# A second seven-product unit beside the first in one tile, weight sums moved between tiles, and two small copies on another engine

## The chip, the cores and the metric

The kernel runs on one core of a Trainium2 chip. The metric is the device time of one execution in microseconds (us). A core has a matrix engine (TensorE, PE in the profile, with its weight loads shown as PEld), a vector engine (VectorE, DVE), a scalar engine (ScalarE, ACT), GpSimd (POOL) and SyncE (SP); each works through its own queue in order, and they wait for each other on semaphores.

## The reference, cut to what matters

Attention over 8 batches of 8 heads, with keys and values pooled by 8 along the sequence, then a feed-forward layer with SiLU between its two products:

```python
k_p = k.reshape(B, H, Sp, 8, D).mean(axis=3)       # B, H, S, D = 8, 8, 576, 64; Sp = 72
v_p = v.reshape(B, H, Sp, 8, D).mean(axis=3)
attn = softmax(q @ k_p.T / sqrt(D))
x = (attn @ v_p) as rows of tokens                  # 4608 x 512
h = x @ w_in                                        # 512 x 2048
g = h * (1.0 / (1.0 + np.exp(-h)))
out = g @ w_out                                     # 2048 x 512, float32
```

## The kernel before

The 4608 tokens are cut into nine tiles of 512, numbered t = 0 to 8. For each tile `up` computes the hidden activations `h_T` (16 groups of 128 hidden units) from `xT`, and `down` or `down_quarters` multiplies them with `w_out` and stores. The attention of the next batch is laid between the matmuls of the current tile.

**The order.** All order is written out by hand. `up` and `down` advance a counter before each small set of matmuls (`next(step)`), and lists of fillers, `f_up` and `f_down`, hold pairs (step, work). `spread` sorts them by step, keeping the order of equals, and issues a filler once the counter has passed its step; what is left is issued at the end. Since every engine takes its work in the order of issue, the step of a filler sets its place in that engine's queue.

**up.** `items` lists what `up` does. A plain group `(g, 0, 512)` is four matmuls of 512 columns into a bank of PSUM, then one SiLU on ScalarE (lines 537 and 543); it counts four steps. The other kind is a unit: four hidden groups (`UNITS`: groups 4 to 7, 8 to 11, 12 to 15) made with seven products instead of eight, in the manner of Strassen and Winograd. In `items` a unit is named by its number and a string of digits, each digit one product of four matmuls of 256 columns (line 477) and two steps. Around the products of a unit stand these operations, in one queue each:

- after 2: ScalarE copies bank P to `r_sb` (line 494); after 5: VectorE adds Q to it, `rr_sb` (497); after 1: VectorE makes `t_sb` from R (500);
- 4 goes on in bank P and 3 in bank Q, each followed by a SiLU from the bank (485);
- 7 goes on in P and 6 in Q, each followed by a VectorE sum into `c_sb[0]` or `c_sb[1]` (509, 512), and "h" and "s" are the SiLUs of those two (485).

Thus 4 waits for the copy, 3 for `rr_sb`, 7 and 6 for the SiLUs of 4 and 3. `r_sb`, `rr_sb`, `t_sb` and `c_sb` exist once and are used by all units. Banks P and Q come from a ring of five ("at"), which the attention uses too, R and the plain groups from a ring of three ("mm"). Tiles 2 to 8 run three units interleaved and four plain groups (the strings `THREE`). Tile 0 has plain groups only. Tile 1 runs one unit (number 0) and twelve plain groups. A unit takes sums of weights, `w_sum1`, built once on VectorE by `unit_weight_sum`: those of units 0 and 1 while tile 0 is in `down`, those of unit 2 in tile 1.

**down.** Tile 0 uses plain products (`down`, line 572). From tile 1 on `down_quarters` uses seven products of 16 matmuls each (line 645), in the order 2, 5, 1, 4, 3, 7, 6, with sums of hidden activations (`h_sum`, `hidden_sum`, line 605, from VectorE) and sums of output weights (`w_sum`, `weight_sum`, line 623). Each weight sum n has PW = 4 parts of two k-groups; its parts are fillers. Sums 1 and 3 are made in tile 0's `down`, sums 4, 7 and 6 in tile 1's `up`. The last tile (`last`) goes over the products 1, 4, 3, 7, 6 twice, once for each half `cc` of its rows; there the bank P is copied to `o_sb[1]` between products 4 and 7 by VectorE (line 667), in the other tiles by ScalarE.

**ScalarE's tables.** `attn_tables` (line 400) loads the set with Exp and Ln, `moe_tables` (403) the set with SiLU; `moe_tables` is issued just before `up`.

**Other lines that are spoken of.** 159: `q_transpose`; 292 and 310: the copies of pooled keys and values to SBUF (`kz`, `vp`); 263 and 267: sums of the loaded rows (`slot_sums`); 393: the attention's result into `xT`; 437, 444: the sums of unit weights and of x; 384: numerators; 358: denominators; 340: scores. `w_out` is loaded in four pieces of four k-groups (`load_w_out`, line 731), pieces 0 to 2 before batch 1's values and piece 3 after them.

Of the kernel before, what the change touches and what calls it, by code (L numbers as in the profile page):

```python
# [36 lines left out]
def kernel(  # L37
# [9 lines left out]
    nc = tc.nc  # L47
# [43 lines left out]
    def ps_tile(shape, dtype, tag, name):  # L91
        return psum.tile(shape, dtype, tag=tag, bufs=banks[tag], name=name)
# [16 lines left out]
    o_sb = [singles.tile([128, 2, d_model], FP32, name=f"o_sb{n}") for n in range(2)]  # L109
# [204 lines left out]
    def part(g, f):  # L314
        return ((g, f * QF, (f + 1) * QF),)
# [36 lines left out]
    def denominators(b, segs, on_dve=False):  # L352
        st = batches[b]
        w = width(segs)
        es = st["es", segs]
        den_ps = ps_tile([128, 512], FP32, "at", "den_ps")
        for s in range(4):
            nc.tensor.matmul(  # L358
                den_ps[32 * s : 32 * (s + 1), :w],
                lhsT=ones, rhs=es[:, s, :], start=True, stop=True,  # L360
            )
        rec = mid.tile([128, VW], FP32, tag="rec", bufs=4, name="rec")[:, :w]
        if on_dve:
            nc.vector.reciprocal(rec, den_ps[:, :w])
        else:
            lnd = mid.tile([128, VW], FP32, tag="lnd", name="lnd")[:, :w]
            nc.scalar.activation(lnd, den_ps[:, :w], func=AF.Ln)  # L367
            nc.scalar.activation(rec, lnd, func=AF.Exp, scale=-1.0)
        st["rec", segs] = rec
# [32 lines left out]
    def moe_tables():  # L402
        nc.scalar.preload_act_table_set("silu_and_others")


    def spread(fillers, n):
        todo = sorted(fillers, key=lambda f: f[0])
        for i in range(n):
            yield i
            while todo and todo[0][0] <= i:  # L410
                todo.pop(0)[1]()
        for f in todo:
            f[1]()
# [28 lines left out]
    def unit_x_sum(t, n):  # L442
        a, b = U_X[n]
        nc.vector.tensor_tensor(  # L444
            out=x_sum[:, U_XI[n]], in0=x_quarter(t, *a), in1=x_quarter(t, *b),
            op=ALU.subtract if n in (3, 4) else ALU.add,
        )
# [97 lines left out]
    def store(t, m, cs, engines=(nc.sync,)):  # L545
        n0 = (t * NTT + m * 128) // QP
        src = o_sb[m // 2][:, m % 2, cs]
        if n0 // QI == B - 1:
            engines[0].dma_start(out=out[n0 * QP : n0 * QP + 128, cs], in_=src)  # L549
            return  # L550
        for u in range(128 // QP):
            n = n0 + u
            rows = (
                out[n * QP : (n + 1) * QP] if n // QI == B - 1
                else out_r[n // QI, n % QI]
            )
            engines[u % len(engines)].dma_start(
                out=rows[:, cs], in_=src[QP * u : QP * (u + 1)]
            )
# [27 lines left out]
    LO, HI, FULL = slice(0, CQ), slice(CQ, 2 * CQ), slice(0, 2 * CQ)  # L587
# [30 lines left out]
    PW = 4  # L618
# [6 lines left out]
    def left(n, kt, c):  # L625
        cs = slice(128 * c, 128 * (c + 1))
        if n in h_sum:
            return h_sum[n][:, kt, cs]
        i = n - 3
        return h_T[:, i * KQ + kt, i * NQ + 128 * c : i * NQ + 128 * (c + 1)]  # L630

    def down_quarters(t, fillers, last=False):
        step = spread(fillers, 7 * 2 * KQ)
        ps = {
            n: ps_tile([128, 2, CQ], FP32, "mm", f"o_ps{n}") for n in "PQR"
        }
        bank = {2: "P", 5: "Q", 1: "R", 4: "P", 3: "Q", 7: "P", 6: "Q"}
        begun = set()

        def product(n, k0, k1, cs=(0, 1)):  # L640
            b = bank[n]
            for kt in range(k0, k1):
                for c in cs:
                    next(step)
                    nc.tensor.matmul(  # L645
                        ps[b][:, c, :], lhsT=left(n, kt, c), rhs=W_OUT[n][:, kt, :],
                        start=b not in begun,
                        stop=kt == k1 - 1, skip_group_check=True,
                    )
                    begun.add(b)  # L650

        add, sub = ALU.add, ALU.subtract
        tt = nc.vector.tensor_tensor
        KA = KQ // 2
        product(2, KA, KQ)
        product(5, KA, KQ)
        product(2, 0, KA)
        nc.scalar.copy(r_sb, ps["P"])
        product(5, 0, KA)
        tt(out=rr_sb, in0=ps["Q"], in1=r_sb, op=add)  # L660
        for cc in ((0,), (1,)) if last else ((0, 1),):
            cs = slice(cc[0], cc[-1] + 1)
            product(1, 0, KQ, cc)
            tt(out=t_sb[:, cs], in0=ps["R"][:, cs], in1=rr_sb[:, cs], op=sub)
            product(4, 0, KQ, cc)
            copy = nc.vector.tensor_copy if last else nc.scalar.copy
            copy(o_sb[1][:, cs, LO], ps["P"][:, cs])
            tail = last and cc == (1,)
            if tail:
                store(t, 3, LO, (nc.gpsimd,))  # L670
            product(3, 0, KQ, cc)
            nc.vector.tensor_copy(out=o_sb[0][:, cs, HI], in_=ps["Q"][:, cs])
            if tail:
                store(t, 1, HI)
            product(7, 0, KQ, cc)
            tt(out=o_sb[0][:, cs, LO], in0=ps["P"][:, cs], in1=t_sb[:, cs], op=add)
            for c in cc:
                store(t, c, LO if tail else FULL, (nc.scalar if tail else nc.sync,))
            product(6, 0, KQ, cc)
            tt(out=o_sb[1][:, cs, HI], in0=ps["Q"][:, cs], in1=t_sb[:, cs], op=add)  # L680
            for c in cc:
                if tail:
                    store(t, 3, HI, both)
                else:
                    store(t, 2 + c, FULL, (nc.gpsimd if last else nc.sync,))
        for _ in step:
            pass
# [105 lines left out]
    for t in range(NT):  # L793
        a = t + 1
        f_up, f_down = [], []
        if t == 0:
            GA = 11
            items = [(g, 0, HS) for g in range(GA)]
            items += [(g, HS, NTT - HS) for g in range(GA)]
            items += [(g, 0, NTT) for g in range(GA, KG)]  # L800
            f_up += [(1, lambda: denominators(0, part(0, 1), on_dve=True))]
            f_up += [(5, lambda: denominators(0, part(1, 1), on_dve=True))]
            f_up += [(13, lambda: numerators(0, part(0, 1)))]
            f_up += [(17, lambda: numerators(0, part(1, 1)))]
        else:
            G = lambda *gs: [(g, 0, NTT) for g in gs]
            if t == 1:
                items = (
                    G(12, 13, 14, 15) + [(0, "251")] + G(8) + [(0, "43")] + G(9)
                    + [(0, "7h6")] + G(10) + [(0, "s")] + G(11, 0, 1, 2, 3)  # L810
                )
            else:
                items = []
                for it in THREE[t // B].split():
                    items += [(("BCA".index(it[0])), it[1])] if it[0] in "ABC" else G(int(it[1]))
            if t == 1:
                for n in U_X:
                    f_up.append((0, lambda n=n: unit_x_sum(t, n)))
            for n in (2, 5):
                h_at = 50 if t == B else 54 if t > 1 else 45  # L820
                f_up.append((h_at, lambda n=n: hidden_sum(n, 4, 8)))
            f_up.append((56, lambda: hidden_sum(6, 4, 8)))
            for n, k0 in ((2, 0), (5, 0), (1, 4), (1, 0)):
                f_up.append((64, lambda n=n, k0=k0: hidden_sum(n, k0, k0 + 4)))
            f_down.append((33, lambda: hidden_sum(7, 0, 8)))
            f_down.append((71 if t < B else 50, lambda: hidden_sum(6, 0, 4)))

        for n, t0, f_to, at, parts in (
            (1, 0, f_down, 48, (0, PW)), (3, 0, f_down, 52, (0, PW)),
            (4, 1, f_up, 38, (0, PW)), (7, 1, f_up, 42, (0, PW)),  # L830
            (6, 1, f_up, 60, (0, PW)),
        ):
            for i in range(*parts):
                if t == t0:
                    f_to.append((at + i, lambda n=n, i=i: weight_sum(n, i)))
# [63 lines left out]
        if t == 1:  # L899
# [5 lines left out]
            f_down.append((72, unit_weight_tiles))  # L905
            for i, n in enumerate(U_W):
                f_down.append((73 if i < 2 else 81, lambda n=n: unit_weight_sum(2, n)))
        moe_tables()
        up(t, f_up, items)
        if t == 0:  # L910
            down(t, f_down, [(0, 1, 2), (3,)])
        else:
            down_quarters(t, f_down, last=t == NT - 1)
# [28 lines left out]
```

The softmax here doesn't subtract the row's maximum and nothing guards it: scores larger than these inputs give would overflow.

## Time and profile before

| what | value |
|---|---|
| median of 6 runs | 280.61 us (280.35 to 281.25) |
| the profiled execution | 280.63 us, of which the span is 278.6 us |
| granted TensorE clock | 1.000 |
| busy share PE / PEld | 98% / 73% |
| busy share DVE / ACT / POOL | 79% / 68% / 35% |
| chain that ended last, PE's share | 94% |
| tile 0's `down`, tile 1's `up`, tile 1's `down` | about 32.6 to 50.9, 50.9 to 65.0 and 65.0 to 81.2 us |

The time of an execution is the span (first to last instruction) and about 2 us around it. Lines of the timeline are: start, duration, engine, source line and operation, output and inputs by the program's names, form, count, and in brackets the idle time before it with what ended that. In the lines of waits the three numbers are the total, the count and the longest. In the chain each line is a start, a length and what the chain went through.

### The profile page before, as it was taken

What the parts mean: (1) busy time and instruction counts of PE and PEld (TensorE: products, weight loads), DVE (VectorE), ACT (ScalarE), POOL (GpSimd) and SP (SyncE); (2) the same over time, 40 slices, a digit from 0 to 9 for tenths busy, and PEclk for the clock granted to TensorE, in tenths of its full rate; (3) what the DMA queues carried; (4) which work ended last, traced back from release to release, by engine and by line L of the source; (5) the groups of instructions that cost most, each with busy time, mean ns of one, the idle gap of its engine ahead of it and who ended that gap; (6) DMA issues with size and microseconds to landing.
All of it is one profiled execution on the core that took longest, in us unless ns stands there. A gap on an engine that the chain in (4) does not pass through costs nothing.

```text
span 278.6 us, 7101 instructions
## 1 busy us (share of the span) xinstructions
PE 272.7 (98%) x2845; PEld 202.9 (73%) x2865; DVE 218.8 (79%) x413; ACT 188.2 (68%) x366; POOL 98.3 (35%) x104
## 2 busy tenths in 40 slices
PE   8999999999999999999999999999999999999995
PEld 4448444556778677867888788687877778788784
DVE  4886737889998976897689768986888588966983
ACT  1688765668577966797679757985799478326700
POOL 8745217332148430953086107970630000000001
PEclk9999999999999999999999999999999999999999
DMA  7999999897669878669755835599610041005004
GB/s 215 276 254 244 207 326 195 227 186 116 133 84 211 216 111 149 143 175 136 135 141 152 129 57 133 142 126 134 145 46 2 2 107 46 0 12 141 1 7 146
DMA packets 31312, 37.70 MB, mean 135 GB/s; under 512 B 10352, under 2 KB 22256, under 8 KB 31280
## 3 DMA queue, kind: packets, MB, share of 16 engines
q0 software_dynamic: 23920, 27.03, 52.5%
q1 hardware_dynamic: 6928, 9.58, 12.3%
q10 hardware_dynamic: 432, 0.66, 0.7%
q8 instruction: 22, 0.36, 0.5%
q14 instruction: 10, 0.08, 0.1%
HBM read 36.70 MB, written 9.44 MB: 166 GB/s over the span
## 4 chain that ended last, share of the span: by engine, by line
PE 94%; DVE 2%; ACT 1%; issue 1%; DVEq 0%
PE hp_ps L537 16%; PE o_psP L645 16%; PE o_psQ L645 16%; PE u_psQ L477 10%; PE u_psP L477 10%; PE o_psR L645 5%; PE sc_ps L340 4%; PE o_ps L572 3%; PE u_psR L477 3%; PE warm_ps L694 3%; PE nu_ps L384 3%; PE den_ps L358 2%; PE warm_ps L698 1%; DVE w_sum L623 1%; DVE xT L393 1%
## 5 line engine op out<-in xcount | busy, mean ns | idle before, releaser
L645 PEld LDWEIGHTS <-h_sum 128*128 128x128 bf16 x640 | 60.6, 98 | 11.9 <-DVE h_sum L605 1.5
L537 PE MATMUL hp_ps<-xT,w_in_sb 128*128 128x512 bf16 (+3 forms) x269 | 51.4, 332 | 1.0 <-issue 0.2
L605 DVE TENSOR_TENSOR h_sum<-h_T 128x1024 bf16<-128x1024 bf16 (+1 forms) x72 | 49.7, 744 | 0.0
L477 PEld LDWEIGHTS <-w_sum 128*128 128x128 bf16 x440 | 43.0, 98 | 7.8
L348 ACT ACTIVATE es<-sc_ps 72x384 bf16<-72x384 f32 (+1 forms) x100 | 39.0, 469 | 8.5 <-PE sc_ps L340 8.3
L543 ACT ACTIVATE h_T<-hp_ps 128x512 bf16<-128x512 f32 (+2 forms) x67 | 33.8, 524 | 11.5 <-PE hp_ps L537 9.8
L537 PEld LDWEIGHTS <-w_in_sb 128*128 128x128 bf16 x284 | 27.0, 98 | 17.1 <-issue 1.1
L485 ACT ACTIVATE h_T<-c_sb 128x512 bf16<-128x512 f32 x44 | 27.5, 628 | 3.1 <-DVE c_sb L509 2.4
L393 DVE TENSOR_TENSOR xT<-nu_ps,rec 128x384 bf16<-128x384 f32 (+1 forms) x50 | 24.0, 533 | 4.3 <-PE nu_ps L384 4.3
L645 PEld LDWEIGHTS <-h_T 128*128 128x128 bf16 x256 | 24.1, 98 | 4.5 <-issue 0.9
L549 POOL DMA_DIRECT2D out_dram<-o_sb x2 | 1.2, 617 | 68.2 <-issue 67.4
L367 ACT ACTIVATE lnd<-den_ps 128x384 f32<-128x384 f32 (+1 forms) x23 | 11.1, 483 | 20.0 <-PE den_ps L358 20.0
L190 POOL TENSOR_TENSOR raw<-raw 72x1024 f32<-72x1024 f32 x10 | 23.6, 2360 | 0.1
L500 DVE TENSOR_TENSOR t_sb<-u_psR,rr_sb 128x512 f32<-128x512 f32 x22 | 15.2, 692 | 7.0 <-PE u_psR L477 5.5
L494 ACT COPY r_sb<-u_psP 128x512 f32<-128x512 f32 x22 | 12.9, 585 | 10.0 <-PE u_psP L477 8.7
L263 DVE TENSOR_TENSOR raw<-raw 128x384 f32<-128x384 f32 (+3 forms) x20 | 12.4, 618 | 8.6 <-DMA raw<-in_v_dram 4.8
L477 PEld LDWEIGHTS <-w_in_sb 128*128 128x128 bf16 x176 | 16.9, 98 | 2.3
L645 PE MATMUL o_psP<-w_out_sb,h_sum 128*128 128x256 bf16 x128 | 17.6, 273 | 0.0
L497 DVE TENSOR_TENSOR rr_sb<-u_psQ,r_sb 128x512 f32<-128x512 f32 x22 | 15.0, 680 | 2.9 <-ACT r_sb L494 1.6
L509 DVE TENSOR_TENSOR c_sb<-u_psP,t_sb 128x512 f32<-128x512 f32 x22 | 15.1, 688 | 2.7 <-PE u_psP L477 1.0
L512 DVE TENSOR_TENSOR c_sb<-u_psQ,t_sb 128x512 f32<-128x512 f32 x22 | 15.1, 687 | 2.3 <-PE u_psQ L477 2.2
L196 POOL COPY gate<-x_sum 1x1 bf16<-1x1 bf16 x5 | 0.9, 180 | 45.3 <-DVE x_sum L444 45.3
(84 smaller groups left out, 525.8 us busy)
## 6 DMA issues: line engine op xcount, KB each, us to landing
out_dram<-o_sb SPq DMA_DIRECT2D x128, 64.0 KB, 1.7
raw<-in_k_dram POOLq DMA_DIRECT2D x10, 576.0 KB, 8.0
raw<-in_v_dram POOLq DMA_DIRECT2D x10, 576.0 KB, 7.8
q_bf<-in_q_dram POOLq DMA_DIRECT2D x6, 576.0 KB, 10.7
w_in_sb<-in_moe_w_in_dram POOLq DMA_DIRECT2D x8, 256.0 KB, 8.7
w_out_sb<-in_moe_w_out_dram POOLq DMA_DIRECT2D x4, 512.0 KB, 13.2
raw<-in_v_dram POOLq DMA_DIRECT2D x2, 768.0 KB, 10.9
raw<-in_k_dram POOLq DMA_DIRECT2D x1, 768.0 KB, 10.8
```

The source lines that it names most:

```text
L190: nc.gpsimd.tensor_add(out=raw[:, :, : 2 * D], in0=raw[:, :, : 2 * D], in1=raw[:, :, 2 * D :])
L348: nc.scalar.activation(es[:, s, :], sc[s], func=AF.Exp, scale=score_scale)
L393: nc.vector.tensor_mul(out=xT[:, 2 * g0 + c : 2 * (g0 + ng - 1) + c + 1 : 2, cols], in0=nu[c][:, :w].rearrange("r (g n) -> r g n", g=ng), ...
L477: nc.tensor.matmul(ps[y, bank][:, u, :], lhsT=w[:, kk, 128 * u : 128 * (u + 1)], rhs=x[:, kk, :], start=first and u == 0 and kk == 0, stop ...
L485: nc.scalar.activation(h_T[:, g : g + 2, j * NQ : (j + 1) * NQ], src, func=AF.Silu)
L500: tt(out=t_sb, in0=ps[y, "R"], in1=rr_sb, op=ALU.subtract)
L509: tt(out=c_sb[0], in0=ps[y, "P"], in1=t_sb, op=ALU.add)
L512: tt(out=c_sb[1], in0=ps[y, "Q"], in1=t_sb, op=ALU.add)
L537: nc.tensor.matmul(hp_ps[:, r0:r1], lhsT=w_in_sb[:, kk, g * 128 : (g + 1) * 128], rhs=xT[:, kk, x0 : x0 + r1 - r0], start=(kk == 0), stop= ...
L543: nc.scalar.activation(h_T[:, g, n0 : n0 + n], hp_ps[:, :n], func=AF.Silu)
L605: nc.vector.tensor_tensor(out=h_sum[n][:, ks, :], in0=quarter(*a, ks), in1=quarter(*b, ks), op=op)
L645: nc.tensor.matmul(ps[b][:, c, :], lhsT=left(n, kt, c), rhs=W_OUT[n][:, kt, :], start=b not in begun, stop=kt == k1 - 1, skip_group_check= ...
```

## The change

Tile 1 runs unit 1 beside unit 0, so that four plain groups fewer (8 to 11) remain; its `items` are a new order. Of the output weight sums, all of 6 and the first halves of 4 and 7 are issued in tile 0's `down`, at steps 8 to 15, and the second halves of 4 and 7 in tile 1's `down`, at steps 22, 23 and 54, 55; none is left in tile 1's `up`. The load of the SiLU tables for tile 1 is issued at step 46 of tile 0's `down` instead of after it. In the last tile ScalarE makes the copies of line 667.

```diff
@@ down_quarters
-            copy = nc.vector.tensor_copy if last else nc.scalar.copy
-            copy(o_sb[1][:, cs, LO], ps["P"][:, cs])
+            nc.scalar.copy(o_sb[1][:, cs, LO], ps["P"][:, cs])
@@ for t in range(NT), t == 1
                 items = (
-                    G(12, 13, 14, 15) + [(0, "251")] + G(8) + [(0, "43")] + G(9)
-                    + [(0, "7h6")] + G(10) + [(0, "s")] + G(11, 0, 1, 2, 3)
+                    G(12, 13, 14, 15) + [(0, "25143"), (1, "2"), (0, "7"), (1, "5")]
+                    + [(0, "6h"), (1, "1"), (0, "s")] + G(0) + [(1, "43")] + G(1)
+                    + [(1, "7h6")] + G(2) + [(1, "s")] + G(3)
                 )
@@ weight sums: (n, tile, list, first step, parts)
             (1, 0, f_down, 48, (0, PW)), (3, 0, f_down, 52, (0, PW)),
-            (4, 1, f_up, 38, (0, PW)), (7, 1, f_up, 42, (0, PW)),
-            (6, 1, f_up, 60, (0, PW)),
+            (6, 0, f_down, 8, (0, PW)), (4, 0, f_down, 12, (0, 2)),
+            (7, 0, f_down, 14, (0, 2)), (4, 1, f_down, 20, (2, PW)), (7, 1, f_down, 52, (2, PW)),
@@
-        moe_tables()
+        if t != 1:
+            moe_tables()
+        if t == 0:
+            f_down.append((46, moe_tables))
         up(t, f_up, items)
```

## The prediction

> **What bounds the kernel now.** First the page: engine shares and the chain that ended last.
>
> ```profile
> PE 272.7 (98%) x2845; PEld 202.9 (73%) x2865; DVE 218.8 (79%) x413; ACT 188.2 (68%) x366; POOL 98.3 (35%) x104
> ...
> PE 94%; DVE 2%; ACT 1%; issue 1%; DVEq 0%
> ```
>
> TensorE's queue is the chain, at full clock, so an edit counts only if it takes TensorE work away or changes one of its waits. The change touches four places: tile 0's `down` (32.6 to 50.9 us), tile 1's `up` (50.9 to 65.0), tile 1's `down` (65.0 to 81.2), the last tile's `down`. I read the timeline of each. Tile 0's:
>
> ```profile
> 30.68 3.40 DVE L437 TENSOR_TENSOR w_sum<-w_in_sb 128x512 bf16<-128x512 bf16 x10
> ...
> 37.01 0.73 POOL L151 DMA_DIRECT2D q_bf<-in_q_dram  x1 [2.00 <-DMA w_out_sb<-in_moe_w_out_dram]
> ...
> 38.92 1.55 DVE L263 TENSOR_TENSOR raw<-raw 128x768 f32<-128x768 f32 x2 [4.84 <-DMA raw<-in_v_dram]
> ...
> 46.56 0.59 ACT L580 COPY o_sb<-o_ps 128x512 f32<-128x512 f32 x1
> ```
>
> VectorE ends the ten unit weight sums at 34.08 and is idle for 4.84 us until batch 1's values land. GpSimd's wait shows that the third piece of `w_out` was there by 37.01. After 47.15 ScalarE is idle for 3.97 us.
>
> Then tile 1's `up`, VectorE and ScalarE (a later mean over several instructions hides their spacing, which is given below):
>
> ```profile
> 55.28 0.58 ACT L494 COPY r_sb<-u_psP 128x512 f32<-128x512 f32 x1
> ...
> 57.30 0.51 DVE L292 CAST kz<-kz_ps 128x144 bf16<-128x144 f32 x2
> 57.73 1.19 DVE L159 STREAM_TRANSPOSE qT<-q_bf 128x288 f32<-128x288 f32 x3
> 59.63 0.69 DVE L509 TENSOR_TENSOR c_sb<-u_psP,t_sb 128x512 f32<-128x512 f32 x1 [0.71 <-ACT h_T L485]
> ...
> 66.65 2.50 DVE L605 TENSOR_TENSOR h_sum<-h_T 128x1024 bf16<-128x1024 bf16 x4
> ```
>
> TensorE does not wait in this `up` after 52.0. But VectorE falls behind: from 59.63 to the end of `vp` at 73.43 it has no idle time, and in tile 1's `down` TensorE waits for it twice:
>
> ```profile
> PEld L645 <- DVE h_sum L605: 0.2, 1, 0.2
> PEld L384 <- DVE vp L310: 0.2, 1, 0.2
> ```
>
> At the end, the chain of the last tile and VectorE's copy of line 667:
>
> ```profile
> 268.32 0.87 PE o_psQ L645 x8
> 269.20 0.01 issue
> 269.21 1.03 PE o_psP L645 x8
> 270.24 0.93 PE o_psQ L645 x8
> ```
>
> ```profile
> 268.74 0.42 DVE L667 COPY o_sb<-o_psP 128x256 f32<-128x256 f32 x1
> ```
>
> Eight matmuls take 0.87 (the first line), so 1.03 and 0.93 hold waits of 0.17 and 0.06: product 7 overwrites bank P, which VectorE has read only at 269.16, since it was on `h_sum` of product 7 (267.27 to 268.49) and `t_sb` before.
>
> **Part 1, tile 0's down: nothing.** Eight weight sums at 0.336 spacing (of 0.42 each, overlapped; 2.76 for eight at 46.67) take 2.7 of the idle 4.84. The four of sum 6 need pieces 0 and 1 of `w_out`, the other four piece 2: in the worst case from 37.01, 4 x 0.336 and one tail, to 38.4; batch 1's values are awaited until 38.92. Behind stand the values' sums and then `select_v`, for which TensorE has 0.66 us more (sums end 42.25, select at 42.91). Without that cover it would be up to 2.7 us. The table load moves past the copies of row blocks 2 and 3 on ScalarE. It delays the first and its stores on SP by 1.28 us, to 48.4; the bank is wanted for a group after 50.9 and `o_sb[1]` after 74, so nobody waits. It starts tile 1's first SiLUs 0.9 us sooner, but TensorE did not wait for those: the SiLU of the fourth group (54.79) already waited for TensorE, as would the copy to `r_sb` at 55.28. Worth 0.
>
> The Trainium skill (ScalarE: Activation LUTs, What ACT_TABLE_LOAD costs) speaks of a drain of about 1.38 us behind each load, 2.66 us in all. Here the load of line 403 started at 51.72, took 1.28, and the SiLU followed at 53.01, so no drain is seen. By the page the copy would end at 49.9 instead of 48.4, with the same sum.
>
> **Part 2, tile 1's up.** Out: 16 matmuls of 512 columns at 0.216 spacing, 3.45 us. In: 28 of 256 at 0.109, 3.06. TensorE saves 0.39 if it never waits. VectorE loses 12 weight sums (4.0 us), but gains four f32 sums of unit 1 (0.69, next one after 0.60, 0.11 later where it reads the one before); ScalarE gives four SiLUs of plain groups for a copy and four SiLUs.
>
> I walked the three queues with these spacings (ScalarE 0.49, 0.53 after a SiLU from `c_sb`; a semaphore about 0.04). A2, A5, A1 (unit 0 = A, unit 1 = B) end as before, and `t_sb` runs from 56.69. The keys' matmuls (0.43) now fall inside A4, so TensorE passes A3 at 57.20, B2 57.64, A7 58.07, B5 58.51, A6 58.95, B1 59.38, G0 60.25, B4 60.69, B3 61.12, G1 61.99. VectorE: two `kz`, three transposes until 58.8, then c7 of A 58.8, `rr_sb` of B 59.4, c6 of A 60.0 to 60.7, `t_sb` of B 60.6 to 61.3. ScalarE: SiLU of c6 from 60.75, and behind it G0's, which was ready at 60.4, from 61.28, B4's 61.77 to 62.37, B3's to 62.86. So B7 can't start at 61.99 but at 62.42, and B6 after it waits to 62.91: **0.43 + 0.05 us of new waits**. G2 and G3 follow and `down` starts at 65.08 instead of 64.98: **+0.09** net instead of -0.39. The waits are the least known term. Below: 0, if the transposes or sums run more overlapped. Above: every late 0.1 us of c6 is passed on in full; 1.2 if c6 comes 0.75 later than walked (a whole copy of 0.58 and a few hand-overs). I take 0.48, as all its terms are rows of this tile.
>
> **Part 3, tile 1's down.** G3's SiLU ends at about 66.02 and the four sums of `h_sum` start at 66.05 instead of 66.65, since no weight sum stands before them. The wait before `h_sum` goes: spacing of matmuls at 67.2 to 67.4 was 0.207 against 0.109, **-0.10**. Steps 22 and 23 put two weight sums (0.67) before `vp`: it ends at 73.43 - 0.60 + 0.67 = 73.50, and the numerators wait for it: **+0.07** on their time of before. Behind the latter pair (steps 54, 55) stand `xT`, `h_sum` 6 and unit 2's weights; VectorE is then 0.74 us later, and had 0.92 us idle at 76.2, so it is even by the copy at 77.14. The scores at 76.03 need a bank that `xT` frees at 75.2. Together: TensorE comes to the numerators 0.01 sooner (+0.09 - 0.10) and waits there until 0.07 after its time of before, so tile 1 ends **0.07 later**.
>
> **Part 4, last tile.** Product 4's first half ends at 268.33. ScalarE is idle from 266.4; 128x256 f32 lies between its rows of 72x256 (0.359) and 128x512 (0.586), nearer the first: 0.37. So P is free at 268.75 (269.0 at the upper bound), and product 7 could start at 269.04. VectorE's copy of Q moves to 269.34 to 269.76, before product 6 at 269.91. Both waits go: **-0.23**. In the second half nothing waited. ScalarE's store there is behind its copy by over 1 us. The bounds are 0 and -0.23.
>
> **Sum.** Against the profiled execution, 280.63 = 278.65 + 1.98: +0.07 - 0.23 = -0.16, so 280.47; it lies 0.02 over the median of 280.61, so **280.45**. Differences within 0.2% (0.56 us) are about what a measurement of this kernel can tell from no change.
>
> **Rivals.**
> *Faster: unit 1 runs without waits.* -0.39 - 0.10 - 0.23, and some hundredths less wait for `vp`: about -0.75, 279.85. For it: tiles 2 to 8 run three units with no wait of TensorE in `up`. Against: there at most one transpose stands between the sums of units. Chance 0.22.
> *Slower: ScalarE's queue closes in tile 1.* B's copy to `r_sb` stands behind two SiLUs (of A4 and A3), and with VectorE in order the sum `rr_sb` of B takes c6 of A with it, and c6 its SiLU, G0's, B4's and so B7. If this slips by 0.75 beyond the walk (c6 ends at 61.5 or later, the point from which it decides), `up` costs +0.84; `h_sum` starts at 66.80 and `vp` ends at 73.43 + 0.15 + 0.67 = 74.25, so tile 1 ends 0.82 late; less 0.23 at the tail: +0.6, 281.2. Against: the walk has the copy done at 58.5, 0.9 before VectorE is free for it. Chance 0.18.
> *No use of ScalarE's copy:* the tail stays, as product 7 waits elsewhere; +0.07, 280.68. About 0.1, inside "same".
> *Weight sums hold the values back in tile 0:* would need the third piece later than 37.5; the values are behind it on the same queue and landed two microseconds after it. Under 0.03.
>
> **How the numbers follow.** Same: 0.60 (forecast 0.5, dead tail 0.1). Faster 0.22, slower 0.18 are the two waits' ends. The range runs from 279.8 (no waits) to 281.2 (closed queue); the likeliest case alone has 280.2 to 280.75.
>
> **What would show it.** Right: DVE's 4.84 us before line 263 shrinks to under 1.5; in tile 1's `up` TensorE waits about 0.4 us before u_psP of B7, released by ScalarE's line 485; `h_sum` leaves the waits of PEld in tile 1, `vp` stays; `down` of tile 1 starts near 65.1; the last tile's 1.03 and 0.93 become 0.87. Wrong: `down` before 64.7 or after 65.7, or a stall at 38 to 43 us.

## The result, and the profile after

The changed kernel takes **279.98 us** (median of 34 runs, 279.81 to 280.73) against 280.51 of the kernel before (70 runs); the ratio is 0.9981, 95% interval 0.9976 to 0.9986: 0.53 us less, just inside the 0.2% that I called no change. The forecast was 280.45.

The stages can be compared by the starts of TensorE's first instruction in each, read from the timelines of the two profiled executions (us):

| stage | before | after | forecast of the difference |
|---|---|---|---|
| tile 0's `down` | 18.27 | 18.27 | 0 |
| tile 1's `up` | 14.07 | 14.10 | +0.09 |
| tile 1's `down` | 16.17 | 16.13 | -0.02 |
| tiles 2 to 7, tile 8's `up` | 181.75 | 181.75 | 0 |
| tile 8's `down`, to the last matmul | 12.64 | 12.41 | -0.23 |
| last matmul to the end of the span | 3.10 | 3.11 | 0 |
| outside the span | 1.98 | 1.78 | 0 |

The profiled execution after took 280.99 us, above the median, since its first product of tile 0's `down` came 0.79 later (33.44 instead of 32.65). That is in a part of the program that the change does not touch; all times of after below stand 0.79 later than the like ones of before.

Tile 0, timeline of after:

```profile
34.50 1.43 DVE L623 TENSOR_TENSOR w_sum<-w_out_sb 128x512 bf16<-128x512 bf16 x4
...
37.33 1.43 DVE L623 TENSOR_TENSOR w_sum<-w_out_sb 128x512 bf16<-128x512 bf16 x4 [1.40 <-DMA w_out_sb<-in_moe_w_out_dram]
...
39.87 1.55 DVE L263 TENSOR_TENSOR raw<-raw 128x768 f32<-128x768 f32 x2 [1.11 <-DMA raw<-in_v_dram]
```

VectorE's 4.84 us before line 263 have become four weight sums, a wait of 1.40 for the third piece of `w_out`, four more sums and a wait of 1.11. The sums of line 263, which wait for the values to land, start 0.16 later after the first product than before (6.43 instead of 6.27), and TensorE does not feel it: tile 0's `down` takes its 18.27.

Tile 1's `up`, the chain of after around product 7 of unit 1 (B7):

```profile
60.88 0.61 DVE c_sb L512
61.49 0.02 issue
61.51 0.63 ACT h_T L485
62.14 0.48 ACT h_T L543
62.62 0.49 ACT h_T L485
63.12 0.04 issue
63.16 0.60 PE u_psP L477 x4
```

This is the queue of the walk: c6 of unit 0, its SiLU, G0's, B4's, then B7. On VectorE c7 and c6 of unit 0 (lines 509 and 512) stand behind the three transposes:

```profile
58.52 1.19 DVE L159 STREAM_TRANSPOSE qT<-q_bf 128x288 f32<-128x288 f32 x3
59.63 0.65 DVE L509 TENSOR_TENSOR c_sb<-u_psP,t_sb 128x512 f32<-128x512 f32 x1
60.20 0.68 DVE L497 TENSOR_TENSOR rr_sb<-u_psQ,r_sb 128x512 f32<-128x512 f32 x1
60.80 0.67 DVE L512 TENSOR_TENSOR c_sb<-u_psQ,t_sb 128x512 f32<-128x512 f32 x1
```

G1's last matmul gave way at 62.79, so B7 waited 0.37 (walk: 0.43), and B6 0.05 more. The list of waits names the releaser, and `vp` is still there while `h_sum` is gone from TensorE's waits in this tile:

```profile
PEld L384 <- DVE vp L310: 0.2, 1, 0.2
...
PE u_psP L477 <- ACT h_T L485: 0.2, 1, 0.2
```

The last tile, chain and timeline of after (the copy is line 666 now):

```profile
269.99 0.87 PE o_psP L645 x8
270.87 0.87 PE o_psQ L645 x8
```

```profile
269.15 0.37 ACT L666 COPY o_sb<-o_psP 128x256 f32<-128x256 f32 x1 [2.00 <-PE o_psP L645]
```

ScalarE's copy took 0.37 and both waits, 0.17 and 0.06, are gone.

So from tile 0's first `down` product to the end of the span the two profiles differ by 0.23 us, all in the last tile; tile 1 is even (30.23 us in both). What the medians have beyond that was the question for the experiments.

### The profile page after: what moved, and what is told of

Its sections match the earlier page's. It is cut to its first block, busy times and chain, and to the rows that moved or that the text cites. A ratio compares the mean times of both kernels' runs of the same rounds, so it can differ in the third digit from the quotient of the medians.

```text
span 279.2 us, 7140 instructions
## 1 busy us (share of the span) xinstructions
PE 272.1 (97%) x2857; PEld 203.8 (73%) x2877; DVE 220.8 (79%) x415; ACT 189.4 (68%) x369; POOL 98.3 (35%) x104
## 4 chain that ended last, share of the span: by engine, by line
PE 88%; DVE 4%; DMA 3%; ACT 2%; issue 1%; POOL 0%; POOLq 0%; DVEq 0%
PE o_psQ L645 16%; PE o_psP L645 15%; PE hp_ps L537 15%; PE u_psP L477 11%; PE u_psQ L477 10%; PE o_psR L645 5%; PE sc_ps L340 4%; PE o_ps L572 3%; PE u_psR L477 3%; DMA raw<-in_v_dram 3%; PE nu_ps L384 3%; PE den_ps L358 2%; DVE w_sum L623 1%; DVE xT L393 1%; ACT h_T L543 1%
## 5 line engine op out<-in xcount | busy, mean ns | idle before, releaser
L645 PEld LDWEIGHTS <-h_sum 128*128 128x128 bf16 x640 | 60.7, 98 | 11.5 <-DVE h_sum L605 1.3
L477 PEld LDWEIGHTS <-w_sum 128*128 128x128 bf16 x460 | 45.0, 98 | 8.4 <-issue 0.5
L537 PE MATMUL hp_ps<-xT,w_in_sb 128*128 128x512 bf16 (+3 forms) x253 | 47.8, 329 | 0.8
L543 ACT ACTIVATE h_T<-hp_ps 128x512 bf16<-128x512 f32 (+2 forms) x63 | 31.6, 520 | 9.9 <-PE hp_ps L537 7.9
L537 PEld LDWEIGHTS <-w_in_sb 128*128 128x128 bf16 x268 | 25.6, 98 | 15.3 <-issue 1.1
L485 ACT ACTIVATE h_T<-c_sb 128x512 bf16<-128x512 f32 x46 | 28.8, 629 | 4.4 <-DVE c_sb L509 3.1
L500 DVE TENSOR_TENSOR t_sb<-u_psR,rr_sb 128x512 f32<-128x512 f32 x23 | 15.9, 692 | 6.7 <-PE u_psR L477 5.0
L477 PEld LDWEIGHTS <-w_in_sb 128*128 128x128 bf16 x184 | 17.6, 98 | 2.4
L497 DVE TENSOR_TENSOR rr_sb<-u_psQ,r_sb 128x512 f32<-128x512 f32 x23 | 15.7, 681 | 3.5 <-ACT r_sb L494 1.6
L512 DVE TENSOR_TENSOR c_sb<-u_psQ,t_sb 128x512 f32<-128x512 f32 x23 | 15.8, 687 | 2.3 <-PE u_psQ L477 2.1
L509 DVE TENSOR_TENSOR c_sb<-u_psP,t_sb 128x512 f32<-128x512 f32 x23 | 15.8, 686 | 2.2 <-PE u_psP L477 0.9
L645 PE MATMUL o_psQ<-w_sum,h_sum 128*128 128x256 bf16 x128 | 16.7, 273 | 0.0
```

The source lines that it names most:

```text
L477: nc.tensor.matmul(ps[y, bank][:, u, :], lhsT=w[:, kk, 128 * u : 128 * (u + 1)], rhs=x[:, kk, :], start=first and u == 0 and kk == 0, stop ...
L485: nc.scalar.activation(h_T[:, g : g + 2, j * NQ : (j + 1) * NQ], src, func=AF.Silu)
L500: tt(out=t_sb, in0=ps[y, "R"], in1=rr_sb, op=ALU.subtract)
L509: tt(out=c_sb[0], in0=ps[y, "P"], in1=t_sb, op=ALU.add)
L512: tt(out=c_sb[1], in0=ps[y, "Q"], in1=t_sb, op=ALU.add)
L537: nc.tensor.matmul(hp_ps[:, r0:r1], lhsT=w_in_sb[:, kk, g * 128 : (g + 1) * 128], rhs=xT[:, kk, x0 : x0 + r1 - r0], start=(kk == 0), stop= ...
```

## The experiments

Each kernel is compared with runs of the kernel before on the same chip. The theory: tile 1 gives nothing because of B7's wait, the last tile gives 0.23, and the rest is not work of the schedule. The rival: one of the parts gives 0.3 us that the profiled executions don't show.

### Each part alone

```diff
 tail_alone:   only   copy(...) -> nc.scalar.copy(o_sb[1][:, cs, LO], ps["P"][:, cs])
 sums_alone:   only   the five rows of weight sums as in the change
 tables_alone: only   moe_tables at step 46 of tile 0's down
 unit_alone:   only   the new items of tile 1
```

tail_alone: 

> Only the last tile's copies of line 667 go to ScalarE; all else as before. By the walk: both waits of the last tile go, 0.23 us less (ratio 0.9992), and the last tile's chain shows 0.87 in place of 1.03 and 0.93. Rival (the part of the gain that the two profiles do not show lies in the last tile, in its stores or around the span): 0.5 us less (0.9982).

sums_alone: 

> Only the weight sums move: sum 6 and half of 4 and 7 to tile 0's down, the other halves to tile 1's down; tile 1 keeps one unit. By the walk: the wait for h_sum goes (0.10) and the one for vp shrinks by about 0.1: 0.1 to 0.2 us less (0.9993 to 0.9996); tile 0 no longer. Rival (the hidden gain lies in the weight sums): 0.4 to 0.5 less. Third case (tile 0 pays): 0.3 or more slower, with a wait of TensorE at 38 to 44 us.

tables_alone: 

> Only the load of the SiLU tables moves from behind tile 0's down to its step 46. By the walk: nothing (1.0000), as TensorE does not wait for the first SiLUs. Rival (most executions, other than the profiled one, do wait for those SiLUs): 0.3 us less (0.9990).

unit_alone: 

> Only tile 1's items change: unit 1 beside unit 0, with the weight sums 4, 7 and 6 still in that up and the tables and the copies as before. By the walk: eight parts of sums 4 and 7 (2.7 us) stand on VectorE before the hidden sums and c7 of unit 1, four of sum 6 before the last hidden sums, so h_sum comes about 1.9 us late for product 2's second half: 1.5 to 2 us slower (1.005 to 1.007). Rival (weight sums were no load): same as before within 0.1.

| kernel | median us | ratio to before (95%) | tile 0 `down` | tile 1 `up` | tile 1 `down` | tile 8 `down` | last matmul to end of span | outside the span |
|---|---|---|---|---|---|---|---|---|
| tail_alone | 280.52 | 0.9999 (0.9991 to 1.0008) | 18.27 | 14.06 | 16.16 | 12.41 | 3.68 | 1.79 |
| sums_alone | 280.44 | 0.9997 (0.9988 to 1.0005) | 18.78 | 14.07 | 16.00 | 12.71 | 3.11 | 1.98 |
| tables_alone | 280.40 | 0.9999 (0.9991 to 1.0008) | 18.27 | 14.06 | 16.16 | 12.64 | 3.10 | 1.94 |
| unit_alone | 282.10 | 1.0058 (1.0046 to 1.0070) | 18.27 | 14.10 | 17.90 | 12.64 | 3.10 | 1.79 |

(The stages are from each kernel's profiled execution, the time outside the span is the mean of time less span over all its runs.)

**The unit alone** costs 1.76 us in tile 1, as walked. The weight sums left in its `up` hold VectorE until the last hidden sums, which start at 68.30 instead of 66.65:

```profile
66.96 1.43 DVE L623 TENSOR_TENSOR w_sum<-w_out_sb 128x512 bf16<-128x512 bf16 x4
68.30 2.49 DVE L605 TENSOR_TENSOR h_sum<-h_T 128x1024 bf16<-128x1024 bf16 x4
```

So moving the sums is what makes the second unit affordable. **The sums alone** take 0.17 out of tile 1's `down`, as expected; the list of waits there has neither `h_sum` nor `vp`. Their time shows little of it. In the profiled execution tiles 2 to 8 took 0.14 more (181.82 and 12.71), for a reason that was not looked for, and tile 0's `down` was 0.51 longer, for which the chain gives the reason:

```profile
27.01 16.17 DMA w_out_sb<-in_moe_w_out_dram
```

TensorE waited for the fourth piece of `w_out`, which landed at 43.19. **The tables alone** do nothing, although the first SiLU came at 52.05 instead of 53.01. **The tail alone** saves its 0.23 before the last matmul and loses 0.58 behind it: its last store landed 2.76 us after the last matmul, in the other three 2.18 or 2.19. It measured as before. The interval excludes the rival's 0.9982 but still holds the 0.9992 of the walk, which had the saving right and knew nothing of the loss. By the means of all runs its span is 0.16 longer than that of the kernel before (278.75 and 278.58), and the time outside the span is 0.19 shorter.

### The changed kernel without its tail, and the tail once more

```diff
 after_no_tail: the changed kernel with
+            copy = nc.vector.tensor_copy if last else nc.scalar.copy
+            copy(o_sb[1][:, cs, LO], ps["P"][:, cs])
 tail_again: tail_alone unchanged
```

after_no_tail: 

> The changed kernel with VectorE's copy back in the last tile: unit, sums and tables remain. Theory (tile 1 is even, the last tile is the gain inside the span): 0.2 us slower than the changed kernel, last tile's chain with 1.03 and 0.93 again; the time outside the span stays at 1.79 if it goes with the unit's program, since the unit alone had 1.79 also. Rival (the tail is worth nothing, as the tail alone measured the same as before): same as the changed kernel, 280.0.

tail_again: 

> The tail alone once more, one look: in its first profile the last store landed 2.27 us after its issue ended beside 1.36 before, 0.58 more than anywhere else, which took the tail's 0.23 back. If that belongs to the kernel, it is there again; if to that execution, the last store lands after 2.18 us from the last matmul, and the span ends 3.1 us after it.

Without its tail the changed kernel takes 280.53 (ratio to before 1.0001, 0.9991 to 1.0011): 0.55 more than with it, where 0.2 was expected. Tile 1 (14.10 and 16.14) is as in the changed kernel, the last `down` 12.64 again, so 0.23 is the tail's. The rest is not in these stages: in its profiled execution tile 0's `down` took 18.58, and by the means of all runs its span is 0.50 longer than that of the changed kernel (278.82 and 278.32). The time outside the span stayed at 1.78, with the unit and without the tail.

The tail once more had its late landing again, at 2.57: it belongs to that kernel. In the trace's DMA packets a single packet of 8 KB of instruction code (queue 14) stands beside it, 1.24 us after the last matmul (1.23 in tail_alone), for 0.56 and 0.72 us. In the kernel before such a packet comes 4.82 us after the last matmul, which is after the span; in the changed kernel 3.67 us before it. Page of before, then of after:

```profile
q14 instruction: 10, 0.08, 0.1%
```

```profile
q14 instruction: 11, 0.09, 0.1%
```

One more piece of code is fetched within the span after the change. Counted over the traces, the packet's place goes with the number of ScalarE's instructions: 444 in before, sums_alone and tables_alone (4.8 to 5.0 after the last matmul); 446 in unit_alone and after_no_tail (4.1 to 4.4 after); 450 in tail_alone (1.2 after); 452 in the changed kernel (3.7 before). And the time outside the span is 1.94 to 1.98 with 444, 1.78 to 1.79 in all of these others. (Instructions of the sequencer are counted.) That gave a new theory: about 0.2 us of the gain is where the last code fetch falls. Whether it falls inside the span can't be what counts, since the span ends 3.10 after the last matmul: in unit_alone and after_no_tail the packet comes behind its end too, and the time outside is 1.79 and 1.78. By the place of the fetch, what counts would be whether it comes by 4.4 us after the last matmul or only at 4.8.

### The code fetch moved by idle copies

```diff
 before_pad: the kernel before, tail_pad: tail_alone, each with
+    pad = singles.tile([128, 1], FP32, name="pad")
+            if t == 0:
+                for _ in range(8):        # 4 in tail_pad
+                    f_down.append((46, lambda: nc.scalar.copy(pad, warm32[:, :1])))
```

before_pad: 

> The kernel before with eight more copies of one column each on ScalarE, at step 46 of tile 0's down, where ScalarE is idle; they compute nothing that is used. Theory (0.19 us of the change's gain is the time outside the span, and goes with where ScalarE's last piece of code is fetched): that time falls from 1.98 to 1.79 us and the last 8 KB packet of code comes before the last matmul, as in the changed kernel; 280.35. Rival (it belongs to the copies of line 667 or to the unit): 1.98 us and 280.55 as before.

tail_pad: 

> The tail alone with four such copies. Theory (in the tail alone the last packet of code, 1.23 us after the last matmul, delays the last store by 0.4 to 0.6): the packet comes before the last matmul, the last store lands 2.18 us after it, the time falls from 280.52 to about 280.1. Rival (the late landing belongs to ScalarE's copy): 280.5 again, landing 2.6 or later.

Half right. In before_pad the packet came 8.7 us before the last matmul and the time outside the span fell from 1.98 to 1.77, with 12.64 in the last tile as before. In tail_pad the packet came 5.9 us before it and the last store landed after 2.18, so the late landing goes with the fetch beside it and not with ScalarE's copy, which stayed. The count alone does not set the place, as these two have 452 and 454 instructions. But neither became faster: 281.10 (ratio 1.0017, 1.0004 to 1.0029) and 280.70 (1.0006, 0.9997 to 1.0015). In their profiled executions tile 0's `down` took 18.77 and 19.39, and the chain of tail_pad has this line:

```profile
27.20 16.26 DMA w_out_sb<-in_moe_w_out_dram
```

The fourth piece of `w_out` landed at 43.77 and 43.46, over a microsecond later than in before (42.28). Whether the new tile, by moving the others in SBUF, or the copies made the early loads slower, was not tried.

### B7's wait taken away

```diff
 late_transposes:  q_at of tile 1  [24, 25, 26, 2] -> [36, 37, 38, 2]
 late_both:        the same, and hidden_sum(7, 0, 8) of tile 1  33 -> 45
 early_transposes: q_at of tile 1  [24, 25, 26, 2] -> [10, 11, 12, 2]
```

late_transposes: 

> The changed kernel, with the three query transposes of tile 1's up at steps 36 to 38 instead of 24 to 26, behind the sums of unit 0 on VectorE. Theory (they hold back c6 of unit 0, and with it the SiLUs that product 7 of unit 1 waits for): TensorE's 0.37 and 0.05 us of waits before B7 and B6 go, tile 1's up takes 13.7 us instead of 14.1, the time falls by 0.4 us to about 279.6. Rival (the wait is ScalarE's own queue, whatever VectorE does): the waits stay, same time.

late_both: 

> As late_transposes, and in tile 1's down the hidden sum of product 7 at step 45 instead of 33, behind the copies of vp. Theory: the wait for vp (about 0.2 us) goes too, so tile 1's down takes 15.9 us instead of 16.1, and the time falls to about 279.4 (ratio to the kernel before 0.996). Rival (what tile 1 gains, later stages give back): tile 2's first product comes sooner but the time stays at 280.0.

early_transposes: 

> The changed kernel with the three query transposes at steps 10 to 12 of tile 1's up, where VectorE has 1.27 us idle before the first rr_sb. Theory: late transposes moved VectorE's delay from c6 of unit 0 to c7 of unit 1 (62.84 in place of 62.4) and so to the last SiLUs and the denominators' wait; early ones cost nothing, so tile 1's up takes 13.68 us as with late ones, and tile 1's down 16.0 instead of 16.13: 0.55 us less than the changed kernel, about 279.45. Rival (TensorE's time in tile 1 is conserved, what up gains down gives back, as with late transposes): 280.0 to 280.2.

| kernel | median us | ratio to before (95%) | tile 0 `down` | tile 1 `up` | tile 1 `down` |
|---|---|---|---|---|---|
| changed kernel | 279.98 | 0.9981 (0.9976 to 0.9986) | 18.27 | 14.10 | 16.13 |
| late_transposes | 280.20 | 0.9986 (0.9977 to 0.9995) | 18.50 | 13.68 | 16.67 |
| late_both | 279.81 | 0.9971 (0.9961 to 0.9981) | 18.42 | 13.68 | 16.26 |
| early_transposes | 279.58 | 0.9969 (0.9958 to 0.9980) | 18.27 | 13.67 | 16.14 |

All three take 0.42 out of tile 1's `up`: the wait was VectorE's, through the three transposes before c7 and c6 of unit 0, and ScalarE's queue only passed it on. That is the theory. But late transposes only move the delay: they and the hidden sums then stand before c7 of unit 1, as the timeline of late_transposes shows:

```profile
60.83 1.19 DVE L159 STREAM_TRANSPOSE qT<-q_bf 128x288 f32<-128x288 f32 x3
61.94 1.25 DVE L605 TENSOR_TENSOR h_sum<-h_T 128x1024 bf16<-128x1024 bf16 x2
63.11 0.68 DVE L509 TENSOR_TENSOR c_sb<-u_psP,t_sb 128x512 f32<-128x512 f32 x1
```

So the last SiLUs, the Exp of the scores and `vp` come late, and tile 1's `down` gives back 0.54. With `h_sum` 7 behind `vp` it still gives back 0.13, by the denominators' wait, where 15.9 was expected for this `down`. The early place costs nothing. Timeline of early_transposes:

```profile
54.30 1.19 DVE L159 STREAM_TRANSPOSE qT<-q_bf 128x288 f32<-128x288 f32 x3
55.65 0.69 DVE L497 TENSOR_TENSOR rr_sb<-u_psQ,r_sb 128x512 f32<-128x512 f32 x1 [0.16 <-ACT r_sb L494]
```

The transposes fill an idle stretch of 1.27 us before the first `rr_sb`; 0.16 is left of it. Tile 1's `down` was expected to fall to 16.0 and stayed at 16.14: TensorE comes 0.42 sooner and waits for `vp` as before (0.2 in the list). Against the changed kernel this one takes 0.40 less by the medians (0.34 by the ratios to the kernel before) and 0.42 less by the stages of tile 1. From late_both it differs by 0.13 in tile 1's stages; their ratios to the kernel before, 0.9969 and 0.9971, don't tell the two apart.

### All sums in tile 0

```diff
 whole_sums: the changed kernel with
+            (6, 0, f_down, 8, (0, PW)), (4, 0, f_down, 12, (0, PW)), (7, 0, f_down, 16, (0, PW)),
```

whole_sums: 

> The changed kernel, but with all four parts of sums 4 and 7 in tile 0's down (steps 12 to 19). The last four need the fourth piece of w_out, which landed at 42.3 in the profile before, behind batch 1's values. Theory: VectorE stands at that wait with the sums of the values behind it, these end at about 47 instead of 42.2, TensorE waits for select_v, and the time grows by 3.5 us (2.5 to 4.2). Rival (the sums in tile 0 hold nothing up): 0.1 us less than the changed kernel, as tile 1's down then has no weight sums ahead of vp.

286.09 us, ratio 1.0195 (1.0171 to 1.0220). The mechanism is the expected one:

```profile
42.65 2.10 DVE L623 TENSOR_TENSOR w_sum<-w_out_sb 128x512 bf16<-128x512 bf16 x6 [5.04 <-DMA w_out_sb<-in_moe_w_out_dram]
...
46.66 0.50 PE L303 MATMUL v_ps<-v,shifts 128*128 128x64 bf16 x6 [3.40 <-DVE v L267]
```

VectorE stands 5.04 us, TensorE then 3.40 for the values. But tile 0's `down` took 24.73, 6.46 more. The windows by time show the other 3 us, in the granted clock, the third number from the end (before it stand the busy times of the five engines; the first window has the wait):

```profile
43.00:46.60 3.60, 0.26 (x2) 0.00 (x0) 3.53 (x10) 0.68 (x2) 2.71 (x3) 0.86 0.90 160
46.60:48.00 1.40, 1.34 (x9) 0.75 (x10) 1.33 (x5) 0.00 (x0) 1.22 (x2) 0.50 1.05 160
48.00:50.00 2.00, 2.00 (x12) 0.72 (x9) 0.74 (x2) 0.59 (x1) 1.12 (x2) 0.50 1.00 157
```

The trace has TensorE at half clock from 45.57 to 52.40, and its matmuls of 512 columns 0.427 apart instead of 0.216. TensorE's last matmul before the wait had ended at 43.26. Of the 6.83 us at half clock, 1.09 were still the wait; the work of the other 5.74 would take half of that at full clock. So about 2.87 us are lost there, an estimate from these times, which is most of the 3 us. Leaving the second halves of sums 4 and 7 to tile 1 is thus what keeps that wait out of tile 0, and tile 1's `down`, at 16.00, shows what they cost there: 0.13. Without them `vp` ends 7.75 us after the start of that `down` instead of 8.41.

## Why the prediction was right or wrong

- **Tile 0, nothing:** right in all three terms. The cover of 4.84 us held, with 1.11 left at its end; whole_sums shows what it is worth where the fourth piece is asked for. The table load is worth nothing (tables_alone). The copy behind the moved load ended at 48.52 on the scale of before, where 48.4 was forecast; 1.38 more than the forecast would have been 49.8, not 49.9, and was not seen.
- **Tile 1's up, +0.09:** right. Measured +0.03; the two new waits were 0.37 and 0.05 against 0.43 and 0.05, so `down` began at 65.02 on the scale of before instead of 65.08 (64.98 + 0.09 is 65.07; the walk rounds). That the saving of 0.39 sits under them is shown by the three kernels with other transposes, which got 0.42 back.
- **Tile 1's down, -0.10 and then +0.07 after the wait for `vp`:** the first is right. `h_sum` left the waits, and the second denominators come 8.08 us after the start of this `down` instead of 8.20. The second was 0.07 too large: `vp` stayed among the waits but ended at 73.43 on the scale of before, as it did before, and not at 73.50, because the 0.06 by which `up` ended sooner than walked was handed on through the hidden sums. Over the two stages of tile 1 the difference is 0.00, forecast +0.07.
- **Last tile, -0.23:** right to 0.01.
- **The sum, -0.16:** too small. Inside the span it was -0.23 by the profiled stages, and by means of all runs -0.26 (278.32 of 35 runs after, 278.58 of 29 of the kernel before in the first experiments). Besides tile 1's +0.07, the mis-sized term is the one that the sum carried over unread: "280.63 = 278.65 + 1.98". The time outside the span became 1.78. That this 0.2 needs neither the unit nor the tail is shown by before_pad, where eight idle copies on ScalarE alone brought it to 1.77. That it goes with the place of the last code fetch fits every kernel here, but the number of ScalarE's instructions fits as well (444 where it is 1.94 to 1.98, 446 or more in all others), and no run separates the two; that these instructions move the fetch is a reading of the traces: in the two padded kernels they did, but by more than the count says. The 0.23 and 0.20 together are 0.43, inside the interval of the 0.53 (0.39 to 0.67).
- **The range:** 279.98 lies in it (279.8 to 281.2), but below the 280.2 to 280.75 that the likeliest case was given. Its walk held and its time did not: that the result still falls inside is luck, owed to the room left for a rival that did not come.
- **The rivals:** neither open case came. *No waits in tile 1* is what early_transposes makes true: from tile 1's first product to the last matmul it takes 223.97 us, before 224.63, which is 0.66 less where that rival had 0.75, as the wait for `vp` stays. *ScalarE's queue closes* had the right queue, with c6 ending at 60.7 on the scale of before, as walked, not at 61.5.

## What to carry to other kernels

A product-saving unit pays only if the engine that makes its sums has room at the right places: walk the queues of all three engines in order, with their spacings, since one late sum is handed on through a SiLU queue in full. Here the unit's saving of 0.39 us was lost to such a wait of 0.42. Fill an idle stretch that lies ahead of the chain rather than moving work behind it, where the next stage pays. And before a change of 0.1% is credited to the schedule, compare the stages, the time behind the last matmul and the time outside the span: here the tail's 0.23 us could be seen in the stages in every kernel that had it, while the tail alone measured the same as before.

## What the runs showed of the hardware

- **Code loading at the end.** With one 8 KB packet of code 1.2 us after the last matmul, the last store landed 0.4 to 0.6 us later (tail_alone, tail_again). With the packet 4.8 to 5.0 us after it, the time outside the span was 1.94 to 1.98; with the packet at 4.4 or sooner, 1.76 to 1.79. Why is not shown.
- **The early loads.** In every profile but that of whole_sums the first plain group of tile 1 starts at the later of two times: 18.27 us after the first product of tile 0's `down`, or 8.27 after the landing of the fourth piece of `w_out`. The second gives 50.81 for late_transposes (42.54), 50.61 for after_no_tail (42.34), 51.46 for sums_alone (43.19) and 52.04 for before_pad (43.77); measured 50.81, 50.61, 51.45 and 52.04. The landing varied between 42.2 and 43.8 in these executions, while in before (42.28) the two times are 50.92 and 50.55, so 0.4 us of lateness is enough to be seen. That this makes the spread between runs of one kernel is likely but not shown, as each kernel has one trace (the tail alone has two).
- **The clock.** A wait of 3.40 us in whole_sums halved TensorE's granted clock for 6.83 us and so cost about twice its length. The Trainium skill (TensorE: Matmul & The Clock Gate, Part 1: The HAM clock gate) says that an idle window of about 3.4 us drops the clock to half and that a busy one restores it. The trace agrees in the length, 6.83 us being two such windows; but the clock dropped 2.31 us after the last matmul had ended (43.26 to 45.57), before 3.4 us of idle time had passed, so here a shorter idle time was enough. My expectation for that kernel, 3.5 us, lacked this term.
